# A retention block and four experts on one core: the order of all engines fixed by hand, attention placed between given expert groups, weights behind the first pairs

## The chip, the cores and the metric

The kernel runs on one core of a Trainium2 chip. The metric is the device time of one execution in microseconds (us). A core has five engines, which the profiles show running side by side, each in the order of its own instruction stream: PE (matmuls; its weight loads are listed as PEld), DVE, ACT and POOL (elementwise work), and SP, which here only issues DMAs. Matmul results land in PSUM and are taken out by DVE or ACT. Time zero is the start of the profiled execution. "Tile" below means 512 tokens of the second stage, "batch" one of the eight batches of the first, "pair" two attention heads.

## The reference, cut to what matters

```python
# q, k, v: (B=8, H=8, S=576, D=64) f32
scores = scale * np.matmul(q, k.transpose(0, 1, 3, 2))
gamma = 1.0 - 2.0 ** (-5.0 - np.arange(H))
Dmat = np.where(rel >= 0, gamma[:, None, None] ** rel[None], 0.0)   # causal decay
attn = np.matmul(scores * Dmat[None], v)
x = attn.transpose(0, 2, 1, 3).reshape(B * S, H * D)                # (4608, 512)
p = domain_probs / (domain_probs.sum(-1, keepdims=True) + 1e-09)    # (4608, 4)
for e in range(4):                                                  # w1: 512x1024, w2: 1024x512
    out += p[:, e:e + 1] * (np.maximum(x @ w1[e], 0.0) @ w2[e])
```

There is no softmax, so attention is done in chunks of 128 positions with a running state (`kv`). The 4608 tokens make nine expert tiles. A batch has 576 tokens, so tile n needs batches up to n: while tile n is in the experts, batch n+1 goes through attention.

## The kernel before: the parts that matter

Both kernels have the same units of work for a pair p of a batch: `T` transposes q and k on PE, DVE copies the result (`qkT`); `kv(n)` adds chunk n to the state in PSUM, ACT copies the state (`sbd`); `S` makes the scores, DVE masks them; `O` makes the outputs, DVE scales them into `xT`. The 64 positions left over after four chunks are the "rests" (`Trem`, `Srem`, `Orem`). An expert takes 12 groups of a tile: 8 first-layer groups of 4 matmuls (`ph`, ReLU on ACT), then 4 second-layer groups of 8 (`po`). A tile so has 48 groups, numbered 0 to 47.

```python
    def mixing_weights():
        nc.sync.dma_start(out=probs, in_=moe_domain_probs.rearrange("(t p) e -> p t e", p=128))
        nc.vector.tensor_reduce(psm, probs, axis=mybir.AxisListType.X, op=ADD)
        # ... cut: + 1e-9, reciprocal, multiply, all on DVE
        def cast_pair(p):                       # f32 -> bf16, inside attention(b)
            h0, h1 = 2 * p, 2 * p + 2
            nc.vector.tensor_tensor(km[:, :, h0:h1, :], t["k"][:, :, h0:h1, :],
                gk[:, 0:NC_, h0:h1].unsqueeze(3).to_broadcast([128, NC_, 2, D]), op=MULT)
            nc.scalar.activation(qm[:, :, h0:h1, :], t["q"][:, :, h0:h1, :], Copy)
            gate[b, p] = nc.gpsimd.tensor_copy(vm[:, :, h0:h1, :], t["v"][:, :, h0:h1, :])
    # ... cut
    att = attention(0)                          # a generator: every yield ends a step
    next(att)
    w = [load_w(0)]                             # w1 and w2 of expert 0, issued on POOL
    after(w[0][0], gate[0, 2])                  # w1 after the v cast of pair 2; w2 is left free
    next(att)
    w += [load_w(e) for e in range(1, E)]
    mixing_weights()
    load_rem(0)
    for i in load(1)[:1]:                       # q, k, v of batch 1, behind expert 0's w2
        after(i, w[0][1])
    # ... cut
        for _ in moe(nt):
            n += 1
            if n == 12 and nt + 2 < B:
                load(nt + 2); load_rem(nt + 2)
            if n >= 3 and n % 2 == 1:
                next(nxt, None)                 # one step of the next batch's attention
```

The tile framework's scheduler takes this program as a proposal: it decides the order on every engine.

## Time and profile before

| stretch | us |
|---|---|
| start, to the first expert matmul | 67.8 |
| tile 0 | 68.2 |
| tiles 1 to 6, each | 63.4 |
| tiles 7 and 8, no attention left | 114.6 |
| span of the profiled run | 631.0 |

The median time is 630.7 us. First the page: busy tenths in 40 slices of 15.8 us each, for PE and for the DMA engines.

```profile
span 631.0 us, 8508 instructions
PE   1410799999999999999999999999999999999997
DMA  9999947451075006500750075000100010001001
```

PE is hardly busy for four slices and solid from the sixth on. The table of waits of PE (who waited for whom: total, times, longest):

```profile
PE s_345 L223 <- DVE qkT L204: 27.0, 1, 27.0
PE pt L201 <- ACT qm L171: 18.0, 4, 8.9
PE s_237 L223 <- DVE qkT L204: 5.3, 1, 5.3
```

All of these fall into the start. The longest leads to DVE. The timeline of DVE at that moment (start, duration, instruction, and in brackets the idle time before it with what ended it), and the list of DMA issues (count, size, us from issue to landing):

```profile
64.38 0.30 DVE L148 TENSOR_REDUCE psm<-probs 128x36 f32<-128x144 f32 x1 [30.61 <-DMA probs<-in_moe_domain_probs_dram]
...
65.23 0.63 DVE L204 COPY qkT<-pt 128x1024 bf16<-128x1024 bf16 x1
...
probs<-in_moe_domain_probs_dram SPq DMA_DIRECT2D x1, 72.0 KB, 37.2
```

The copy that PE wanted stood behind the reduction of the mixing weights, and that one waited for a DMA of only 72 KB that took 37.2 us. It moves 4608 rows of 16 bytes each, beside the weights. The second wait (q casts, 18.0 us, of which 8.9 are for the first data) begins on the SP queue, where the loads of q, k and v are issued:

```profile
8.04 0.51 SPq L79 DMA_DIRECT2D raw_k<-in_k_dram  x1
8.59 8.52 SPq L79 DMA_DIRECT2D raw_v<-in_v_dram  x2
17.15 5.43 SPq L79 DMA_DIRECT2D raw_q<-in_q_dram  x2
```

An issue takes 0.51 us until two weight loads, which the scheduler had moved forward to 6.1 and 10.1 us, come to share the DMA engines; then two issues take 8.52 us.

### The profile page before, as it was taken

How to read it: one execution, taken by the hardware profiler on the slowest of the kernel's cores; microseconds unless marked ns; L12 is line 12 of the kernel's file. 1: busy time of each engine (PE TensorE's matmuls, PEld its weight loads, DVE VectorE, ACT ScalarE, POOL GpSimd, SP SyncE). 2: the span in 40 equal slices, each digit the busy share in tenths (PEclk: the TensorE clock that was granted, in tenths of full speed). 3: DMA queues.
4: the chain of work that ended last, by engine and by line, in shares of the span. 5: the costliest groups of instructions: out<-in, count | busy, mean ns of one | idle time of the engine just before them, and what ended most of it. 6: DMA issues, size and time to landing. Idle time of an engine off the chain costs nothing.

```text
span 631.0 us, 8508 instructions
## 1 busy us (share of the span) xinstructions
PE 568.6 (90%) x3453; PEld 271.2 (43%) x3520; DVE 203.0 (32%) x333; ACT 245.8 (39%) x458; POOL 32.2 (5%) x58
## 2 busy tenths in 40 slices
PE   1410799999999999999999999999999999999997
PEld 0210344445444444445444544444445444444443
DVE  3210424541452145214531463146314430121121
ACT  3310464525433543354335433533353335333332
POOL 3300100010001000100010001000100000000000
PEclk9999999999999999999999999999999999999999
DMA  9999947451075006500750075000100010001001
GB/s 161 189 203 198 209 89 166 111 149 33 1 151 142 1 2 151 143 1 0 151 142 2 1 150 142 1 1 1 66 2 1 1 66 1 2 0 68 0 1 67
DMA packets 130167, 46.77 MB, mean 74 GB/s; under 512 B 119376, under 2 KB 123472, under 8 KB 130128
## 3 DMA queue, kind: packets, MB, share of 16 engines
q1 hardware_dynamic: 123856, 37.84, 26.3%
q0 software_dynamic: 6272, 8.39, 7.7%
q8 instruction: 27, 0.44, 0.3%
q14 instruction: 12, 0.10, 0.1%
HBM read 45.16 MB, written 9.44 MB: 87 GB/s over the span
## 4 chain that ended last, share of the span: by engine, by line
PE 88%; DMA 6%; SPq 4%; issue 1%; DVE 0%; ACT 0%
PE ph L325 40%; PE po L332 39%; DMA probs<-in_moe_domain_probs_dram 6%; SPq L79 4%; PE pt L201 2%; PE o L248 2%; PE o L252 1%; PE kvp L188 1%; PE ptr L210 0%; PE orem L261 0%; PE orem L265 0%; DVE acc L338 0%; DVE qkT L204 0%; PE s_345 L223 0%; ACT sbd_151 L194 0%
## 5 line engine op out<-in xcount | busy, mean ns | idle before, releaser
L327 ACT ACTIVATE hT<-ph 128x512 bf16<-128x512 f32 x288 | 171.6, 597 | 249.9 <-PE ph L325 240.9
L332 PEld LDWEIGHTS <-hT 128*128 128x128 bf16 x1152 | 110.0, 98 | 125.4
L338 DVE SCALAR_TENSOR_TENSOR acc<-po,probs,acc 128x512 f32<-128x512 f32 x108 | 81.1, 751 | 189.1 <-PE po L332 164.6
L325 PE MATMUL ph<-xT,wt_388 128*128 128x512 bf16 x276 | 67.6, 380 | 0.6
L325 PE MATMUL ph<-xT,wt_384 128*128 128x512 bf16 x278 | 67.6, 379 | 0.5
L325 PE MATMUL ph<-xT,wt_380 128*128 128x512 bf16 x278 | 67.6, 379 | 0.5
L325 PE MATMUL ph<-xT,wt_289 128*128 128x512 bf16 x284 | 66.1, 388 | 0.4 <-issue 0.2
L332 PE MATMUL po<-wt_386,hT 128*128 128x512 bf16 x280 | 65.6, 379 | 0.4
L332 PE MATMUL po<-wt_291,hT 128*128 128x512 bf16 x280 | 65.3, 379 | 0.4
L332 PE MATMUL po<-wt_382,hT 128*128 128x512 bf16 x282 | 64.9, 379 | 0.1
L332 PE MATMUL po<-wt_390,hT 128*128 128x512 bf16 x279 | 64.3, 379 | 0.5
L204 DVE COPY qkT<-pt 128x1024 bf16<-128x1024 bf16 x32 | 22.0, 687 | 107.9 <-PE pt L201 107.9
L325 PEld LDWEIGHTS <-wt_289 128*128 128x128 bf16 x288 | 28.3, 100 | 34.4 <-issue 2.4
L336 ACT ACTIVATE acc<-po,probs 128x512 f32<-128x512 f32 x36 | 24.8, 688 | 38.3 <-PE po L332 38.3
L325 PEld LDWEIGHTS <-wt_380 128*128 128x128 bf16 x288 | 26.8, 98 | 28.2
L325 PEld LDWEIGHTS <-wt_384 128*128 128x128 bf16 x288 | 26.7, 98 | 28.2
L325 PEld LDWEIGHTS <-wt_388 128*128 128x128 bf16 x288 | 26.4, 98 | 28.5
L172 POOL CAST vm<-raw_v 128x512 bf16<-128x512 f32 x32 | 19.1, 627 | 375.4 <-PE o L248 347.7
L255 DVE TENSOR_TENSOR xT<-o,gq 128x512 bf16<-128x512 f32 x32 | 22.0, 688 | 25.6 <-PE o L252 25.2
L201 PE MATMUL pt<-ident,qm 128*128 128x128 bf16 x128 | 13.2, 230 | 18.2 <-ACT qm L171 18.0
L168 DVE TENSOR_TENSOR km<-raw_k,gk 128x512 bf16<-128x512 f32 x32 | 20.8, 698 | 23.2 <-DMA raw_k<-in_k_dram 11.2
L223 PEld LDWEIGHTS <-qkT 64*128 64x128 bf16 x256 | 7.7, 98 | 46.8 <-DVE qkT L204 34.7
(225 smaller groups left out, 298.6 us busy)
## 6 DMA issues: line engine op xcount, KB each, us to landing
out_dram<-acc SPq DMA_DIRECT2D x36, 256.0 KB, 2.1
raw_k<-in_k_dram SPq DMA_DIRECT2D x64, 128.0 KB, 3.2
raw_v<-in_v_dram SPq DMA_DIRECT2D x64, 128.0 KB, 3.1
raw_q<-in_q_dram SPq DMA_DIRECT2D x64, 128.0 KB, 3.4
wt_291<-in_moe_w_dram POOLq DMA_DIRECT2D x1, 1024.0 KB, 12.3
wt_380<-in_moe_w_dram POOLq DMA_DIRECT2D x1, 1024.0 KB, 14.1
wt_382<-in_moe_w_dram POOLq DMA_DIRECT2D x1, 1024.0 KB, 11.5
wt_289<-in_moe_w_dram POOLq DMA_DIRECT2D x1, 1024.0 KB, 16.7
```

The costliest lines, as they stand in the source:

```text
L79: ins.append(nc.sync.dma_start(out=t[n][:, :, h, :], in_=main_in(src, b, h)))
L168: nc.vector.tensor_tensor(km[:, :, h0:h1, :], t["k"][:, :, h0:h1, :], gk[:, 0:NC_, h0:h1].unsqueeze(3).to_broadcast([128, NC_, 2, D]), op= ...
L172: gate[b, p] = nc.gpsimd.tensor_copy(vm[:, :, h0:h1, :], t["v"][:, :, h0:h1, :])
L201: nc.tensor.transpose(pt[:, i, c * C:(c + 1) * C], src[:, c, 2 * p:2 * p + 2, :].rearrange("p h d -> p (h d)"), ident)
L204: nc.vector.tensor_copy(qkT[:, :, p, 0:SM], pt)
L248: nc.tensor.matmul(o[64 * j:64 * j + 64, c * C:(c + 1) * C], lhsT=vm[:, c, 2 * p + j, :], rhs=sT[p][:, j, c, :], start=(c == 0), stop=Fals ...
L255: nc.vector.tensor_tensor(xT[:, p, b * S:b * S + SM], o, gq[:, p, 0:SM], op=MULT)
L325: nc.tensor.matmul(ph, lhsT=w1_sb[e][:, dc, fc * 128:(fc + 1) * 128], rhs=xT[:, dc, n0:n0 + NT], start=(dc == 0), stop=(dc == NDC - 1))
L327: nc.scalar.activation(hT[:, fc, :], ph, Relu)
L332: nc.tensor.matmul(po, lhsT=hT[:, fc, ns * 128:(ns + 1) * 128], rhs=w2_sb[e][:, fc, :], start=(fc == 0), stop=(fc == NFC - 1))
L336: nc.scalar.activation(acc[ns], po, Copy, scale=pe)
L338: nc.vector.scalar_tensor_tensor(acc[ns], po, pe, acc[ns], op0=MULT, op1=ADD)
```

## The change

The intent: fix the order on all engines by hand, so that the start is short and no unit of attention is reached before its inputs. The diff cut to its core; most of its length is the attention generator turned into a class whose units are called one by one.

```diff
+    ctx.enter_context(tc.manual_schedule())          # engines keep the order of the program
+    load(0)                                          # q, k, v of batch 0; order k, q, v
+    probs_raw = const.tile([NTT, 128, E], FP32)      # 2 KB rows, transposed on PE below
+    nc.sync.dma_start(out=probs_raw, in_=moe_domain_probs.rearrange("(t p) e -> t p e", p=128))
+    load_rem(0)
     def mixing_weights():
-        nc.sync.dma_start(out=probs, in_=moe_domain_probs.rearrange("(t p) e -> p t e", p=128))
+        pp = ps_at.tile([128, E, NTT], FP32, tag="at", name="pp")
+        for e in range(E):
+            nc.tensor.transpose(pp[:, e, :], probs_raw[:, :, e], identf)
+        nc.vector.tensor_copy(probs, pp)
 # ... cut: units; S and O now take a list of pairs
+    def casts0(p):                                   # batch 0: k on DVE, q on ACT, v on POOL
+        # ... cut
+        if p == 2:
+            load_w1(0)
+            a0.w20 = load_w2(0)
+    for p in allp:
+        casts0(p)
+        if p > 0:
+            a0.O([p - 1])
+        a0.T(p)
+        a0.kv(0, [p])
+        a0.S([p])
+        for n in range(1, NCH):
+            a0.kv(n, [p])
+    for e in range(1, E):
+        load_w1(e)
+        load_w2(e)
+    load(1, a0.w20)
+    load_rem(1)
+    a0.O([3])
+        if nt == 0:                                  # at(g, ...): emit after expert group g
+            at(1, mixing_weights)
+            at(3, lambda: a0.cast_rem(nc.gpsimd))
+            at(9, a0.Trem)
+            # ... cut: Srem at 11, Orem at 13, Att(1) at 14
+            for p, g in zip(allp, (22, 31, 40, 44)):
+                at(g - 4, *[lambda p=p, n=n: state["a1"].cast(n, p, nc.gpsimd) for n in "kqv"])
+                at(g, lambda p=p: state["a1"].T(p), lambda p=p: state["a1"].kv(0, [p]))
+                # ... cut: kv(1), S at g+1; kv(2) at g+2; kv(3), O at g+3
+            at(46, lambda: state["a1"].cast_rem(nc.gpsimd))
+            at(47, lambda: state["a1"].Trem(), lambda: state["a1"].Srem(), lambda: state["a1"].Orem())
+            at(47, lambda: load(2), lambda: load_rem(2))
+        elif nt + 1 < B:
+            at(0, *[lambda p=p, n=n: A.cast(n, p, nc.gpsimd) for n in "kqv" for p in allp])
+            # ... cut: rests cast at 0, next load at 2, kv at 9, 11, 13, 15, T at 17, 19, 21, 23
+                at(27, lambda: A.S([0, 1]))
+                at(32, lambda: A.O([0, 1]))
+                at(36, lambda: A.S([2, 3]))
+                at(40, lambda: A.O([2, 3]))
```

Besides the order: the probabilities travel in long rows, the k and q casts of batches 1 to 7 move from DVE and ACT to POOL, and in the steady tiles S and O are done for two pairs at a time.

## The prediction

> **What bounds the kernel now.** From 68 us on TensorE is solid (the table of engine waits has no later PE wait worth naming). A steady 512-token tile takes 63.4 us (stretch table, 262.8 to 326.2): 256 expert matmuls 55.3 us, one batch's attention 8.1. The last two tiles, without attention, take 114.6 us. The first 68 us are start-up. There PE waits 27.0 us in one piece (S of pair 3 on the copy of qkT): DVE stands at the reduction of the mixing weights, whose DMA (16-byte rows) lands after 37.2 us. Another 18 us are waits for q casts: two weight loads, issued at 6.1 and 10.1 us, hold up pairs 1 to 3.
>
> **What the change does.**
> 1. Probabilities come in 2 KB rows and are transposed on PE: the 27 us wait goes, all of it critical.
> 2. Weights follow pair 2's v cast, so q, k, v land undisturbed: batch 1's load (first issue 63.1 us, last cast 79.1) took 16 us. All pairs should land by 18 us. The first batch is then bound by its own chain (T, copy, S, kv steps 0.80 us apart, next q cast, O): about 6 us a pair, from 7.5 on. First expert matmul near 31 us (67.8 before). Weights land 5.1 us apart; the first should land near 25: no limit.
> 3. S and O run in double units: each switch to half-array matmuls shows a gap of 0.1 us and a like loss within. 0.8 us a tile less, 5 us in all.
> 4. k and q casts move to POOL, where a 128x512 cast takes 0.63 us. The k multiply I estimate at 1.2 us, from the Trainium skill, "GPSIMD Engine Reference", elementwise cycle accounting (4497 ns for 2048 elements, two inputs); no trace shows it yet. 13 us of POOL work per tile: harmless in steady state.
> 5. Costs. At the end of tile 0 Trem, Srem, Orem stand back to back: two exposed DVE round trips, 2 us. Batch 2's load is queued behind tile 0's last output and its casts run all k, all q, all v, so v0 is cast 19 us after tile 0's last group; PE wants it 14 us after (group 9 of tile 1). I expect one PE wait of 5 to 7 us, and 2 us of slow matmuls after it (the Trainium skill, "TensorE: Matmul & The Clock Gate", Part 1: an idle window of 3.4 us; here matmuls after the 27 us wait start 0.43 us apart instead of 0.216 until 74 us).
>
> **Sum.** Start 31; tile 0 with cold start and rests 70; tile 1 with its wait 72; five tiles at 62.6, 313; last two 114.6. About 600 us, 5% faster; range 586 to 613. Chances: faster 0.95, within 2% 0.04, slower 0.01.
>
> **What would show it.** PE solid from slice 3 instead of 5. PE waits: no 27 us wait; a kv wait on POOL's v cast of 5 to 7 us near 110 us; two 1 us waits near 100. Steady tiles 62 to 63 us. q and k casts gone from ACT and DVE. Probabilities land in a few us; weights between 24 and 75 us.
>
> **What would make it wrong.** Tile 1's wait missing (590), or longer through a slow POOL multiply; weights late, sharing DMA with batch 1; a hand-placed unit too close to its inputs, repeated in six tiles (1 us each is 1%); a first chain faster than 6 us a pair.

## The result, and the profile after

| | before | changed |
|---|---|---|
| median of 4 runs | 630.74 us | 603.67 us |
| lowest to highest | 629.31 to 631.13 | 602.53 to 604.67 |

The ratio is 0.957 (95% interval 0.955 to 0.960), so 4.3% faster. Ratios here and below are the mean time of one kernel's fast runs over that of the other's of the same rounds, so not quite the ratio of the medians quoted. "Before" was run again beside every experiment and had medians of 630.7 to 631.3 us. The changed kernel was not run again, so "more" or "less than the changed kernel" below compares medians of different sessions.

The page of the changed kernel:

```profile
span 602.2 us, 8558 instructions
PE   3698898799999999999999999999999999999997
DMA  8999923990039002900191008200100010000001
PEclk9999899889999999999999999999999999999999
```

A slice is now 15.1 us. PE is solid from the third slice on, but slices 4, 5, 7 and 8 are not full, and the granted clock (last line, in tenths) dips in slices 5, 8 and 9. The waits of PE:

```profile
PE kvp L195 <- POOL vm L182: 9.2, 5, 4.3
PE pt L208 <- ACT qm L180: 7.1, 4, 6.5
PE kvp L195 <- ACT sbd_162 L200: 2.3, 5, 0.5
...
PE sr_1079 L251 <- DVE qkT L216: 0.8, 1, 0.8
...
PE orem L281 <- DVE sTr L255: 0.5, 1, 0.5
```

The 27.0 us wait is gone; the q casts cost 7.1 us, of which 6.5 are the wait for the first data. New is a wait of `kv` for POOL's v casts, 9.2 us in five pieces. The timeline of PE has the four largest of those:

```profile
62.66 0.22 PE L195 MATMUL kvp<-vm,km 128*128 128x128 bf16 x1 [4.34 <-POOL vm L182]
...
119.61 0.26 PE L195 MATMUL kvp<-vm,km 128*128 128x128 bf16 x1 [4.02 <-POOL vm L182]
120.17 0.27 PE L195 MATMUL kvp<-vm,km 128*128 128x128 bf16 x1 [0.30 <-POOL vm L182]
120.73 0.27 PE L195 MATMUL kvp<-vm,km 128*128 128x128 bf16 x1 [0.29 <-POOL vm L182]
```

One is in tile 0 at 58 to 63 us, the others in tile 1 at 116 to 121. The table of stretches (stretch, its length, busy time and count of PE, PEld, DVE, ACT, POOL, then granted clock, DMA share, GB/s), for tile 0, tile 1 and a steady tile:

```profile
28.30:103.60 75.30, 68.86 (x433) 32.75 (x440) 23.92 (x42) 28.05 (x68) 12.37 (x17) 0.98 0.79 152
103.60:174.95 71.35, 65.91 (x400) 31.37 (x407) 20.30 (x32) 24.50 (x44) 21.49 (x30) 0.93 0.45 104
174.95:237.47 62.52, 62.10 (x401) 30.47 (x408) 20.64 (x32) 24.40 (x44) 10.74 (x15) 1.00 0.30 75
```

| stretch | before | predicted | changed |
|---|---|---|---|
| start | 67.8 | 31 | 28.3 |
| tile 0 | 68.2 | 70 | 75.3 |
| tile 1 | 63.4 | 72 | 71.35 |
| tiles 2 to 6 | 317.0 | 313 | 312.6 |
| tiles 7, 8 | 114.6 | 114.6 | 114.6 |
| sum | 631.0 | 600.6 | 602.2 |

So 39.5 us came out of the start and 4.4 us out of tiles 2 to 6; 15.0 us were given back in tiles 0 and 1.

### The profile page after: what moved, and what is told of

Its sections match the earlier page's. It is cut to its first block, busy times and chain, and to the rows that moved or that the text cites. A ratio compares the mean times of both kernels' runs of the same rounds, so it can differ in the third digit from the quotient of the medians.

```text
span 602.2 us, 8558 instructions
## 1 busy us (share of the span) xinstructions
PE 569.4 (95%) x3457; PEld 275.1 (46%) x3524; DVE 181.1 (30%) x298; ACT 232.3 (39%) x446; POOL 88.9 (15%) x131
## 4 chain that ended last, share of the span: by engine, by line
PE 85%; DMA 8%; SPq 4%; issue 1%; POOL 1%; ACT 0%; DVE 0%; POOLq 0%
PE po L305 39%; PE ph L298 38%; SPq L80 4%; DMA raw_v<-in_v_dram 4%; DMA wt_276<-in_moe_w_dram 3%; PE pt L208 2%; PE o L265 1%; PE kvp L195 1%; PE o L270 1%; DMA raw_q<-in_q_dram 1%; DMA raw_k<-in_k_dram 0%; PE ptr L215 0%; POOL vm L182 0%; DVE acc L312 0%; PE orem L281 0%
## 5 line engine op out<-in xcount | busy, mean ns | idle before, releaser
L305 PEld LDWEIGHTS <-hT 128*128 128x128 bf16 x1152 | 111.4, 98 | 133.7 <-issue 8.2
L298 PE MATMUL ph<-xT,wt_387 128*128 128x512 bf16 x279 | 66.6, 380 | 0.5
L298 PE MATMUL ph<-xT,wt_274 128*128 128x512 bf16 x279 | 66.4, 394 | 0.6 <-issue 0.2
L298 PE MATMUL ph<-xT,wt_379 128*128 128x512 bf16 x281 | 66.4, 379 | 0.4
L298 PE MATMUL ph<-xT,wt_383 128*128 128x512 bf16 x279 | 65.5, 380 | 0.4
L177 POOL TENSOR_TENSOR km<-raw_k,gk 128x512 bf16<-128x512 f32 x28 | 28.7, 1047 | 201.1 <-PE pt L208 133.5
L298 PEld LDWEIGHTS <-wt_274 128*128 128x128 bf16 x288 | 28.9, 101 | 35.7 <-issue 4.1
L298 PEld LDWEIGHTS <-wt_383 128*128 128x128 bf16 x288 | 26.8, 98 | 30.4 <-issue 0.4
L298 PEld LDWEIGHTS <-wt_387 128*128 128x128 bf16 x288 | 26.8, 98 | 30.1
L298 PEld LDWEIGHTS <-wt_379 128*128 128x128 bf16 x288 | 27.0, 98 | 27.9
L182 POOL CAST vm<-raw_v 128x512 bf16<-128x512 f32 x32 | 18.6, 613 | 95.9 <-PE o L265 75.9
L195 PE MATMUL kvp<-vm,km 128*128 128x128 bf16 x128 | 18.1, 229 | 13.8 <-POOL vm L182 9.2
## 6 DMA issues: line engine op xcount, KB each, us to landing
wt_276<-in_moe_w_dram POOLq DMA_DIRECT2D x1, 1024.0 KB, 17.3
```

The costliest lines, as they stand in the source:

```text
L177: self.gate[n, p] = eng.tensor_tensor(o, i, gk[:, 0:NCH, h].unsqueeze(3).to_broadcast([128, NCH, 2, D]), op=MULT)
L182: self.gate[n, p] = eng.tensor_copy(o, i)
L195: nc.tensor.matmul(self.kvp[:, p, :], lhsT=flat(self.m["k"][:, n, h, :]), rhs=flat(self.m["v"][:, n, h, :]), start=(n == 0 and i == 0), st ...
L298: nc.tensor.matmul(ph, lhsT=w1_sb[e][:, dc, fc * 128:(fc + 1) * 128], rhs=xT[:, dc, n0:n0 + NT], start=(dc == 0), stop=(dc == NDC - 1))
L305: nc.tensor.matmul(po, lhsT=hT[:, fc, ns * 128:(ns + 1) * 128], rhs=w2_sb[e][:, fc, :], start=(fc == 0), stop=(fc == NFC - 1))
```

## The experiments

Twelve kernels ran. They start from either side: repairs added to the kernel before, with the scheduler still in charge, and single parts undone or mended in the changed kernel.

### 1. The probabilities alone

```diff
 # kernel before
-        nc.sync.dma_start(out=probs, in_=moe_domain_probs.rearrange("(t p) e -> p t e", p=128))
+        nc.sync.dma_start(out=probs_raw, in_=moe_domain_probs.rearrange("(t p) e -> t p e", p=128))
+        # four transposes on PE and a copy, as in the changed kernel
```

> The kernel before with one thing changed: the probabilities come in 2 KB rows and are transposed on PE. Theory A (the start-up repairs make the gain, not the hand order): the 27 us PE wait behind the reduction of the mixing weights goes, the first expert matmul moves from 67.8 to about 43 us, the time falls to about 606 us (600 to 612), nearly all of the change. Theory B (the order itself is what is worth it): the scheduler places something else in the gap, or batch 1's casts now wait for DMA on ACT and DVE and hold PE up; the time stays above 618 us.

Measured: 624.78 us (623.76 to 625.22), ratio 0.990. The first expert matmul did move to 42.7 us, 25 us sooner, but only 6.5 us of it came through. Theory A fell. The waits of PE in this kernel:

```profile
PE pt L209 <- ACT qm L179: 16.0, 4, 8.7
PE po L340 <- ACT hT L335: 11.6, 1, 11.6
PE s L231 <- DVE qkT L212: 7.8, 2, 6.9
```

The second line is new. The timeline of ACT shows what ACT was doing while PE waited for a ReLU (`hT`):

```profile
54.83 0.60 ACT L335 ACTIVATE hT<-ph 128x512 bf16<-128x512 f32 x1 [0.61 <-PE ph L333]
68.28 0.63 ACT L179 ACTIVATE qm<-raw_q 128x512 bf16<-128x512 f32 x1 [12.85 <-DMA raw_q<-in_q_dram]
68.81 1.07 ACT L335 ACTIVATE hT<-ph 128x512 bf16<-128x512 f32 x2
```

It stood 12.85 us at the first q cast of batch 1, whose data had not landed, with two ReLUs behind it. The Trainium skill ("TensorE: Matmul & The Clock Gate", specification table) calls ScalarE, VectorE and GpSimdE strict FIFO; the trace agrees, nothing passed the cast. The long probability DMA had hidden this: with PE idle until 68 us, batch 1 was never asked for before it was there.

### 2. The probabilities and the order of the weights

```diff
 # on top of 1
-    after(w[0][0], gate[0, 2])
+    for i in w[0]:
+        after(i, gate[0, 2])
     w += [load_w(e) for e in range(1, E)]
+    for we in w[1:]:
+        for i in we:
+            after(i, gate[0, 3])
```

> As before_probs, and all weight loads held behind the v cast of pair 2 (the first two) and pair 3 (the other six), by dependencies, the scheduler still ordering everything. Theory A: q, k, v land by 18 us, the first expert matmul comes near 31 us, the time is 595 to 602 us, so that the hand order adds nothing over the two repairs. Theory B: it stays above 606 us, with PE waits in tile 0 or 1 that the hand-ordered kernel does not have.

Measured: 619.08 us (618.31 to 619.28), ratio 0.980. The first expert matmul came at 24.8 us, but as in experiment 1 most of the shorter start is lost: the wait for the ReLU behind the q cast grew from 11.6 to 17.3 us.

### 3. The casts on POOL as well

```diff
 # on top of 2, for batches 1 to 7 (rests of batch 0 too)
-            nc.vector.tensor_tensor(km...)
-            nc.scalar.activation(qm..., Copy)
+            nc.gpsimd.tensor_tensor(km...)
+            nc.gpsimd.tensor_copy(qm...)
```

> before_probs_w, and the k and q casts of batches 1 to 7 (and all rests) on POOL, the scheduler still ordering everything. before_probs_w waited 17.3 us in tile 0: a q cast of batch 1 stood in front of the ReLUs on ACT and waited for its DMA. Theory C (three repairs are needed: probabilities, weights, and casts on an engine whose waiting holds nobody up): that wait goes, and the time is 598 to 606 us, what the hand-ordered kernel takes. Rival D: the order by hand is worth more than 5 us over the three repairs; the time stays above 608 us, with PE waits in tile 0 or 1 for units placed by the scheduler.

Measured: 617.37 us (616.12 to 618.72), ratio 0.979. Theory C fell too. ACT no longer waits, but PE does:

```profile
PE pt L212 <- POOL qm L182: 11.8, 1, 11.8
PE pt L212 <- ACT qm L180: 9.6, 3, 8.4
PE kvp L199 <- POOL vm L183: 7.3, 3, 6.2
```

PE meets the transposes of batch 1's first pair at 50.6 us, and the q data are cast only at 61.7 us. PE's order is fixed as well, so it stands there. This led to theory E: what counts is how much expert work lies in each queue in front of the first use of batch 1.

### 4. The place of batch 1, the scheduler still in charge

```diff
 # on top of 3: batch 1 pair by pair, as the changed kernel has it, at the same groups
+        elif b == 1:
+            cast_pair(0)
+            yield
+            for p in range(NP):
+                U_T(p); U_kv(0, [p])             # and cast_pair(p + 1)
+                yield
+                # ... cut: kv(1), S | kv(2) | kv(3), O; after the last pair the rests
-            if n >= 3 and n % 2 == 1:
+            if (n in STEPS) if nt == 0 else (n >= 3 and n % 2 == 1):
                 next(nxt, None)
```

> before_pw_pool (the scheduler orders, probabilities, weights and casts repaired, 617.4 us) with batch 1's attention in tile 0 handed to the scheduler pair by pair at the groups that the changed kernel uses (22, 31, 40, 44). Theory E: its 19 us of PE waits for POOL's casts fall to about 5, and the time to 600 to 606 us, with the scheduler still in charge: the placement is what the hand order had over the three repairs. Rival D: the fixed order on the engines is itself worth it: above 611 us.

Measured: 600.21 us (597.07 to 602.78), ratio 0.951. This is no slower than the hand-ordered kernel, with the scheduler deciding every order. PE's waits for POOL fell from 19 us to one:

```profile
PE pt L212 <- ACT qm L180: 9.5, 3, 8.3
PE pt L212 <- POOL qm L182: 3.5, 1, 3.5
```

Its steady tiles still take 63.4 us, not 62.5. What it saves against the hand-ordered kernel lies before tile 1, which starts at 98.8 us instead of 103.6, and in tile 1, which takes 64.5 us instead of 71.35: it queues batch 2's load at group 12, so that tile 1 has no wait for it (see experiment 7). These figures are from the profiled run, the fastest of its four (597.07 us). The edit also cuts batch 1 into pairs, so place and grouping changed together; the next experiment moves the place alone.

### 5. The same from the other side: batch 1 earlier in the changed kernel

```diff
 # changed kernel
-            for p, g in zip(allp, (22, 31, 40, 44)):
-                at(g - 4, ...casts...)
+            for p, g in zip(allp, (14, 23, 32, 41)):
+                at(g if p == 0 else g - 4, ...casts...)
```

> The changed kernel with batch 1's four pairs placed at groups 14, 23, 32 and 41 of tile 0 instead of 22, 31, 40 and 44, nothing else. Theory E (batch 1's data land at 44 to 78 us whatever the order, as they share the DMA engines with the weights; what counts is how much expert work stands in front of their first use in PE's queue): PE reaches pair 0 some 9.5 us earlier and waits so much longer, about 14 us instead of 4.3; the time rises by 8 to 10 us, to 611 to 614. Rival: the place does not matter, the wait is made up later in the tile: 602 to 606.

Measured: 614.45 us (613.55 to 615.86), ratio 0.974, 10.8 us more than the changed kernel. The waits for pair 0 are 4.87 us (transposes, q cast) and 8.08 us (kv, v cast), 13 us instead of 4.3, and the kv still starts at 62.0 us:

```profile
52.90 0.61 PE L208 MATMUL pt<-ident,qm 128*128 128x128 bf16 x4 [4.87 <-POOL qm L182]
62.02 0.27 PE L195 MATMUL kvp<-vm,km 128*128 128x128 bf16 x1 [8.08 <-POOL vm L182]
```

The data land when they land; theory E stands on both sides. The two undo experiments next show which of the change's other parts matter.

### 6. Undoing parts of the changed kernel

Probabilities in 16-byte rows again:

```diff
-    nc.sync.dma_start(out=probs_raw, in_=moe_domain_probs.rearrange("(t p) e -> t p e", p=128))
+    nc.sync.dma_start(out=probs, in_=moe_domain_probs.rearrange("(t p) e -> p t e", p=128))
```

> The changed kernel with the probabilities again in 16-byte rows. Theory: they land some 37 us or more after their issue at 14 us, the first expert output needs them at about 38 us, and the engines stop until about 52 to 60: the time rises by 12 to 20 us, to 616 to 624. Rival: with the reduction placed after group 1 and the first use at group 8, the hand order hides most of it: below 608 us.

Measured: 616.49 us (613.89 to 617.45), ratio 0.977, 12.8 us more. The size was as expected, the path was not: PE's wait of 16.9 us is for the cast of batch 0's rests, which are loaded right behind the probabilities.

Casts of k on DVE and of q on ACT again:

```diff
+    ENG = {"k": nc.vector, "q": nc.scalar, "v": nc.gpsimd}
-                at(g - 4, *[lambda p=p, n=n: state["a1"].cast(n, p, nc.gpsimd) for n in "kqv"])
+                at(g - 4, *[lambda p=p, n=n: state["a1"].cast(n, p, ENG[n]) for n in "kqv"])
-            at(0, *[lambda p=p, n=n: A.cast(n, p, nc.gpsimd) for n in "kqv" for p in allp])
+            for p in allp:
+                at(2 * p, *[lambda p=p, n=n: A.cast(n, p, ENG[n]) for n in "kqv"])
```

> The changed kernel with the k casts of batches 1 to 7 back on DVE and the q casts on ACT (v stays on POOL), a pair every two groups in the steady tiles. Theory C: in tile 0 ACT stands at q casts that wait for batch 1's load, so the ReLUs and PE stop for about 10 us in all; in the steady tiles the inputs have long landed and little changes (62 to 63.5 us a tile); the time rises to 610 to 620 us. Rival (my prediction's item 4: the move to POOL is neither gain nor loss): 601 to 606 us.

Measured: 600.12 us, but with an unusual spread, 598.11 to 603.60; ratio 0.952. The expected loss did not come. At group 18 ACT reaches the first q cast just as its data land (an idle time of 0.41 us), so it holds up nothing. In tile 1 PE waits 5.2 us for ReLUs behind q casts in place of the 4.9 us for POOL. The profiled run is the slowest of the four (603.60 us); why the other three were faster was not traced. Moving the casts to POOL was no part of the gain; whether it costs a few tenths of a per cent is left open, since the edit also spreads the casts over several groups.

Single pairs for S and O in the steady tiles:

```diff
-                at(27, lambda: A.S([0, 1]))
-                at(32, lambda: A.O([0, 1]))
-                at(36, lambda: A.S([2, 3]))
-                at(40, lambda: A.O([2, 3]))
+                for p, gs, go in zip(allp, (27, 29, 35, 37), (32, 33, 40, 41)):
+                    at(gs, lambda p=p: A.S([p]))
+                    at(go, lambda p=p: A.O([p]))
```

> The changed kernel with S and O of the steady tiles in units of one pair (groups 27, 29, 35, 37 and 32, 33, 40, 41) instead of two. Prediction's item 3: 0.8 us a tile, six tiles, 5 us: 607 to 610 us, steady tiles 63.2 to 63.4 instead of 62.5. Rival: the 0.9 us a tile came from elsewhere (kv and T in a row, no wait near the units): below 605 us.

Measured: 608.59 us (608.02 to 610.21), ratio 0.965, 4.9 us more. Two steady tiles of this kernel in the table of stretches:

```profile
174.95:238.30 63.35, 62.93 (x401) 30.21 (x408) 20.73 (x32) 24.40 (x44) 10.73 (x15) 1.00 0.30 74
238.30:301.70 63.40, 62.98 (x402) 30.23 (x408) 20.73 (x32) 24.40 (x44) 10.73 (x15) 1.00 0.29 73
```

The tile is back at 63.4 us. The whole steady-state gain, 0.9 us a tile, is the pairing of S and O. That it is the switches to half-array matmuls that cost the time, as the prediction has it, was not tested apart from the pairing.

### 7. Batch 2's load in front of the outputs

```diff
-            at(46, lambda: state["a1"].cast_rem(nc.gpsimd))
-            at(47, lambda: load(2), lambda: load_rem(2))
+            at(42, lambda: state["a1"].cast_rem(nc.gpsimd))
+            at(42, lambda: load(2), lambda: load_rem(2))
```

> The changed kernel with batch 2's load queued at group 42 of tile 0, in front of tile 0's outputs instead of behind them. Theory: the four PE waits of tile 1 on POOL's v casts (4.0 and three of 0.3 us near 116 to 121) are due to that place in the queue; they go, with the slow matmuls after them, and the time falls by 6 to 8 us, to about 596. Rival: POOL's 13 us of casts per batch are what is late (the k multiply takes 1.05 us there); then the waits stay, and the time moves by less than 2 us.

Measured: 596.67 us (594.85 to 597.37), ratio 0.945, 7.0 us less than the changed kernel. The four waits of tile 1 are gone; one wait for a v cast is left, that of tile 0:

```profile
PE kvp L195 <- POOL vm L182: 5.6, 1, 5.6
```

In the changed kernel's SP queue batch 2's load stood behind the four outputs of tile 0:

```profile
94.69 6.57 SPq L314 DMA_DIRECT2D out_dram<-acc  x4
101.35 1.02 SPq L80 DMA_DIRECT2D raw_k<-in_k_dram  x2
```

Here it starts at 77.83 us. POOL's casts (k multiply 1.05 us each) are fast enough; the load was late. The wait of tile 0 was 5.6 us in this run instead of 4.3, and tile 0 took 76.2 us instead of 75.3; tile 1 fell from 71.35 to 64.2.

### 8. The weights of experts 2 and 3 later

```diff
-    for e in range(1, E):
-        load_w1(e)
-        load_w2(e)
+    load_w1(1)
+    load_w2(1)
     # in tile 0, with the casts of pairs 0 and 1 of batch 1:
+                if p < 2:
+                    at(g - 4, lambda p=p: load_w1(p + 2), lambda p=p: load_w2(p + 2))
```

> The changed kernel with the weights of experts 2 and 3 issued after batch 1's pair 0 and pair 1 casts instead of all at 17 to 21 us. Theory: the 4.3 us PE wait in tile 0 (kv of pair 0 on POOL's v cast, at 58 us) comes from batch 1's load sharing the DMA engines with six weight matrices (two issues took up to 8.7 us on the SP queue); it goes, with the slow matmuls after it, and the time falls by 5 to 6 us, to about 598. Rival: the load starts too late at 31.8 us whatever shares the engines; then the wait stays, or expert 2's weights come late and PE waits there instead.

Measured: 598.64 us (597.94 to 598.71), ratio 0.948, 5.0 us less. The wait of tile 0 is gone and no wait for weights came: in the profiled run tile 0 took 68.6 us instead of 75.3. Tile 1 took 72.3 instead of 71.35, as its longest wait for a v cast grew from 4.0 to 6.0 us. In the changed kernel the SP queue's timeline shows batch 1's load held up while six weight matrices are under way:

```profile
31.77 1.11 SPq L80 DMA_DIRECT2D raw_k<-in_k_dram  x2
32.97 3.32 SPq L80 DMA_DIRECT2D raw_q<-in_q_dram  x2
36.39 8.66 SPq L80 DMA_DIRECT2D raw_v<-in_v_dram  x2
45.09 8.45 SPq L80 DMA_DIRECT2D raw_k<-in_k_dram  x2
```

With the weights spread, the same four lines take 0.95, 3.00, 4.27 and 4.01 us. That fits the Trainium skill ("DMA: Bandwidth & Descriptors", Queues, rings and completion order), which has each DMA engine go round-robin over its queues a packet at a time; no run here shows that mechanism itself, only that the two queues slow each other.

### 9. All repairs together

Experiments 7 and 8, and two more repairs: batch 1's rests go into tile 1 (after groups 1, 3 and 5), and batch 0's pairs overlap by one.

```diff
+    casts0(0)
+    a0.T(0)
     for p in allp:
+        if p + 1 < NP:
+            casts0(p + 1)
         a0.kv(0, [p])                # first try: kv(0, [p + 1]) stood before kv(3, [p])
         a0.S([p])
         a0.kv(1, [p])
+        if p + 1 < NP:
+            a0.T(p + 1)
         a0.kv(2, [p])
         a0.kv(3, [p])
```

> The changed kernel with four repairs: batch 2's load at group 42 (as after_load2), the weights spread (as after_w_spread), batch 1's rests moved into groups 1, 3 and 5 of tile 1, and batch 0's pairs overlapped by one (T of the next pair between the kv steps of this one). If the gains are separate: 603.7 - 7 - 5 - about 2.5 (two PE waits of 0.8 and 0.5 us and some slow matmuls) - about 4 (first expert matmul near 24.5 us instead of 28.3) = about 585 us. Rival: the repairs overlap or uncover the weights (the first matrix landed at 24.2, the second at 31.7 us), and the time stays above 590.

The first try took 585.33 us but its result was wrong (relative error 0.064). I had let the next pair's kv step 0, which starts a new accumulation, run before this pair's step 3; all pairs share one PSUM bank. The Trainium skill ("PSUM — Partial Sum Buffer", The four PSUM rules) says that a starting matmul clears the accumulate bits of the whole bank, so the older sum is overwritten by its next step.

> after_best with its mistake mended: there kv step 0 of the next pair, which starts a new accumulation in the shared PSUM bank, stood before kv step 3 of this pair; now it stands after it. Correct, and 584 to 588 us: the four repairs add up, 15 us or more below the changed kernel's 603.7. Rival: the mended order costs the start-up gain back (first expert matmul at 28 us again), 588 to 591 us.

Mended: 585.07 us (584.55 to 585.53), correct, ratio 0.927 to before. The wrong result went with that one move, as the rule says it should. This kernel beats both: 18.6 us less than the changed one. Its page and its waits:

```profile
PE   4799999999999999999999999999999999999997
...
PE pt L208 <- ACT qm L180: 6.5, 1, 6.5
PE kvp L195 <- ACT sbd L200: 3.6, 7, 0.7
PE kvp L195 <- POOL vm L182: 1.0, 1, 1.0
```

No wait longer than 1.0 us is left after the first data. The first expert matmul starts at 25.5 us instead of 28.3. Experiments 7 and 8 give 12.0 us of the 18.6 and the start 2.8; the remaining 3.8 I put down mainly to moving the rests (two waits of 0.78 and 0.50 us and about 1.5 us of slow matmuls after them, see the last section), but no run moved them alone. A rival for part of it: experiments 7 and 8 each left the other tile 0.9 us longer, and with both repairs together neither loss appears (tile 0 takes 66.4 us, tile 1 64.1).

## Why the prediction was right, and where it was not

The time (600 predicted, 603.7 measured) and the sum of stretches were right, and most terms were. That the sum came so close is partly luck: the start was 2.7 us shorter than its term, and tile 0 5.3 us longer.

**Start: right.** 31 us predicted, 28.3 measured. The chain of batch 0's pairs was slightly mis-sized: "about 6 us a pair" was 5.44 (transposes at 6.50, 11.94, 17.38, 22.82 us), and it began 1.0 us sooner than the 7.5 us of the prediction. The first two weight matrices landed at 24.2 and 31.7 us and did not bind.

**"The 27 us wait goes, all of it critical": only half right.** The wait went, but experiment 1 shows that removing it alone gives 6.5 us, not 27. Behind it stood the next wait, for batch 1's data. In the changed kernel the gain came through because batch 1 is used late (experiments 4 and 5). The prediction did not see that the place of batch 1 was what the start's gain depended on; undoing the probabilities in the changed kernel costs 12.8 us.

**Tile 0: the term that was off.** 70 us predicted, 75.3 measured. The prediction had the weights wait for batch 1 ("weights late, sharing DMA with batch 1") as a risk. It was the other way round: batch 1 waited for the weights, PE stood 4.34 us for a v cast, and the group of matmuls after that (seven recorded) took 3.07 us instead of the 1.89 of the later groups. Experiment 8 removed it and saved 5.0 us.

**Tile 1: right in size, with one term missing.** Predicted were a wait of 5 to 7 us for the v casts at group 9, and 2 us of slow matmuls. PE's waits there are 4.9 us in four pieces (6.2 us from stop to start with the matmuls between), and the 15 recorded matmuls after it take 4.85 us instead of 3.40 (the same count at 139.05 us). Another 1.5 us was not foreseen: the first expert layer of the tile took 8.54 us instead of 7.07 (see the last section). Experiment 7 moved one load and saved 7.0 us. The two waits at the end of tile 0 were predicted as 1 us each and measured 0.78 and 0.50.

**Steady tiles: right.** 62.6 predicted, 62.52 measured, and experiment 6 shows that the pairing of S and O is the cause.

**Casts on POOL: right.** "Harmless in steady state": no wait after tile 1. The k multiply was estimated at 1.2 us from the skill's page and takes 1.05. That the move also gained nothing is shown by undoing it.

**What the hand order itself is worth.** The prediction costed the parts and left this open. Experiment 4 answers it: with the same placement of batch 1 and the same three repairs the scheduler's order takes 600.2 us. That is not quite a like for like comparison: the scheduled kernel lacks the pairing of S and O, which is worth 4.9 us, and also the late load of batch 2, which costs 7.0 us. But a fixed order as such is not needed for the gain; it was the means to write the placement down.

## What to carry to other kernels

When one long wait at the start is removed, ask at once which data the engines will now reach sooner than before, and when those land: an engine takes its instructions in order, so a cast or a transpose that waits for a DMA stops all the work behind it (12.85 us in experiment 1, 11.8 us in experiment 3). Place the first use of such data behind enough ready work, and give urgent loads a place in the DMA queues ahead of those whose users come later. Then look for the seams, such as the change from one tile to the next, where a hand-made plan puts two dependent steps back to back.

## What the Trainium skill lacked or had wrong

- "TensorE: Matmul & The Clock Gate", Part 1, gives the slow clock in its table of states after an idle window of about 3.4 us; further on, under a second failure mode, it tells of frequent short idle times, without durations. In the changed kernel the clock fell after waits of only 0.78 and 0.50 us at the end of tile 0: in the 3.6 us from 100.0 to 103.6 us PE was busy 2.12 us, the granted clock was 0.59 in the next 3.4 us, and the next expert layer (31 matmuls recorded) took 8.54 us instead of the 7.07 of a steady tile. With the same two waits the kernel of experiment 8 kept a granted clock of 1.00, and its layer took 7.07 us; the other five profiled kernels that have these waits show 0.54 to 0.62. So a stretch of small matmuls with short waits can be enough but is not always; where the limit lies, these runs do not say.
- The granted clock of the profile does not show a cold start: in the kernel before it reads 1.00 in the first 80 us, while matmuls near 70 us start 0.43 us apart instead of 0.216. Here the cold start has to be read from the spacing; no page names this case.
- "GPSIMD Engine Reference", section 3.1: scaling its 4497 ns for 2048 elements to 512 gives an estimate of 1.1 us, I allowed 1.2, and a 128x512 multiply with a broadcast operand took 1.05 us. The page has no figure for float32 in and bfloat16 out.
- "DMA: Bandwidth & Descriptors" has no figure for 16-byte rows: 4608 of them took 37.2 us beside weight loads in the kernel before, and 33.2 us in the changed kernel with them put back.
- The same page does not say how much a stream of short rows loses beside large weight loads: two issues of 256-byte rows took 8.7 us instead of 1.05.
